# Padding that starts both operands of the large products at one remainder of 512 bytes

## The chip, the cores and the metric

One core of a Trainium2 chip runs the kernel as one program. The metric is device microseconds (us) of one execution. The five engines are TensorE (PE in the rows; its weight loads are PEld), VectorE (DVE), ScalarE (ACT), GpSimd (POOL) and SyncE (SP). On-chip memory is addressed by bytes along each of 128 partitions; a tile starts at the same byte in each of them.

## What is computed

The reference, cut to its three stages:

```python
attn = softmax(q @ mean8(k).T * scale)          # 8 x 8 heads, 576 rows, 72 pooled keys
x = attn @ mean8(v)                             # to 4608 tokens x 512
idx = argmax(xn @ en.T / tau)                   # one of 8 experts for each token
out[idx == e] = gate * (relu(x[idx == e] @ w1[e]) @ w2[e])   # 512 -> 1024 -> 512
h = out @ w_in                                  # 512 -> 2048
return (h * cos(h)) @ w_out                     # 2048 -> 512
```

## The kernel before

Each large product is done three times over split operands: a float32 operand is cast to the tile `hi` (type fp32r), and `lo` is what the cast lost; hi·hi, lo·hi and hi·lo are summed in PSUM. A product instruction has a stationary operand of 128 x 128 elements, which a weight load (LDWEIGHTS) brings in, and a moving operand of 128 x 512 elements. Each product has a weight load of its own, and TensorE fetches the next one while a product runs.

After attention (to about 215 us) come 41 items of 128 tokens of one expert. `gemm1` (line 707) multiplies the transposed tokens `xh`/`xl` (stationary) with expert weights in `slot` (moving): 24 products for an item. `t_h` (719) transposes the result, and `gemm2` (730) multiplies `h0h`, `h0l`, `h1h`, `h1l` (stationary) with `slot` (moving), again 24. The order on TensorE is gemm1 of item i, four transposes of the next item's tokens (686), gemm2 of item i-1, eight transposes of item i's result. VectorE makes the hi and lo tiles (679, 680), the relu (710) and, between items, converts feed-forward weights.

From about 737 us the feed-forward stage runs over 9 groups of 512 tokens with 16 steps in each, 144 steps. A step has 12 products in `ff1` (854): the stationary operand is a piece of `slot` (the first weights), the moving one is `x2`, the group's transposed tokens. Then come 12 products of `ff2` (880) for the step two before: `gh`/`gl` are stationary, `slot` (the second weights) is moving. Between them `act` makes gh and gl of a step: ScalarE writes `u` (864), VectorE takes off the whole turns through `nr` (865, 866), ScalarE takes the sine (867), VectorE multiplies with the result in PSUM (868) and writes gh and gl (869, 870). x2 alternates between two places, `x2a` for even groups and `x2b` for odd ones.

Where the built program places these tiles, in bytes of the partition, before and after the change:

| tile | used as | start before | remainder of 512 | start after | remainder of 512 |
|---|---|---|---|---|---|
| slot (131072 bytes) | moving in gemm1, gemm2, ff2; stationary in ff1 | 21632 | 128 | 21632 | 128 |
| xh, xl | stationary in gemm1 | 175456, 177504 | 352, 352 | 175744, 177792 | 128, 128 |
| h0h, h0l, h1h, h1l, gh, gl | stationary in gemm2 and ff2 | 152704 and on by 2048 | 128 | the same | 128 |
| x2a | moving in ff1, even groups | 200672 | 480 | 200704 | 128 |
| x2b | moving in ff1, odd groups | 175456 | 352 | 175744 | 128 |
| u (two), nr | work tiles of act | 196576, 198624, 194528 | 480 | 196224, 198272, 194176 | 128 |
| h | relu's result, transposed by t_h | 179552 | 352 | 179840 | 128 |

All pieces of these operands lie at multiples of 512 bytes from the start of their tile, so a piece has the remainder of its tile. u, nr and h are not padded themselves: they lie beside tiles that are.

Of the kernel before, what the change touches and what calls it, by code (L numbers as in the profile page):

```python
# [8 lines left out]
F32 = mybir.dt.float32  # L9
F32R = mybir.dt.float32r  # L10
# [12 lines left out]
def attention_moe_ffn_kernel(  # L23
# [21 lines left out]
    KC = DM // 128  # L45
    FC1 = F1 // 128
# [3 lines left out]
    XW = DM + 2  # L50
# [8 lines left out]
    def pool(name, bufs, es=ctx, **kw):  # L59
        return es.enter_context(tc.tile_pool(name=name, bufs=bufs, **kw))  # L60

    const = pool("const", 1)
    wes = ExitStack()
    rawp = [pool("rawa", 3, side="right"), pool("rawb", NB - 3, wes, side="right")]
    dram = pool("dram", 1, space=DRAM)
# [3 lines left out]
    def bank(i, name):  # L69
        return psp[0].tile([128, 512], F32, tag=f"p{i}", name=name)  # L70
# [38 lines left out]
    W_GROUP = "expert_weights"  # L109
    sem_raw = [tc.alloc_semaphore(f"raw{i}") for i in range(NB)]  # L110

# [3 lines left out]
    def w_load(j, eng=nc.scalar):  # L115
        e, c = order[j]
        t = rawp[j % NB > 2].tile([128, QW], F32, tag="raw", name="raw")
        src = (w1 if c < 4 else w2)[e].rearrange("(p k) n -> p (k n)", p=128)
        d = eng.dma_start(t, src[:, (c % 4) * QW:(c % 4 + 1) * QW])
        d.then_inc(sem_raw[j % NB], 16)  # L120
        tc.no_tile_sem_insts.add(d.ins.name)
        tc.add_to_no_dep_group(f"raw_load{j}", d.ins)
        raws[j] = t

    def w_hi(slot, j):
        e, c = order[j]
        s = ((e + 1) % 2) * SLOT
        hi = slot[:, s + c * QW:s + (c + 1) * QW]
        lo = slot[:, s + HALF + c * QW:s + HALF + (c + 1) * QW]
        nc.scalar.wait_ge(sem_raw[j % NB], 16 * (j // NB + 1))  # L130
        i = nc.scalar.activation(hi, raws[j], AF.Copy)  # L131
        tc.declare_no_dep(i.ins, group=f"raw_load{j}", reason="waits for the load's own semaphore")
        tc.declare_fence(i.ins, group=f"raw_load{j}")
        tc.add_to_no_dep_group(W_GROUP, i.ins)
        raws[j] = raws[j], hi, lo
# [72 lines left out]
    def scatter(n):  # L208
        xt = XT.pop(n)
        nc.gpsimd.tensor_copy(xt[:, DM:XW], GT[:, n, :])  # L210
        apart("xv_rows", nc.gpsimd.indirect_dma_start(
            out=xv, out_offset=bass.IndirectOffsetOnAxis(ap=DESTI[:, n:n + 1], axis=0),
            in_=xt, in_offset=None,
        ))


    def phase_a(es, xtp, zero):
# [277 lines left out]
        def step(n):  # L495
# [88 lines left out]
            if n >= 0 and n % 9 == 8:  # L584
                for j in range(NB // 4):
                    w_load(n // 9 * (NB // 4) + j)
# [63 lines left out]
    def experts_and_feed_forward(slot, wes):  # L650
        htp = pool("hTp", 1)
# [3 lines left out]
        xtp = pool("xTp", 1, bes)  # L655
# [15 lines left out]
            else:  # L671
                d = nc.sync.dma_start(X[i], xv[0:128, :])

        def halves(pl, tg):
            return [pl.tile([128, 4, 128], F32R, tag=tg + t, name=tg + t) for t in "hl"]

        def split(p, hi, lo):
            pv = p.rearrange("p (k n) -> p k n", k=4)
# [141 lines left out]
        Y, X2 = {}, {}  # L820
# [6 lines left out]

        def t_y(g, r, b):
            if r == 0:
                X2[g] = x2p[g % 2].tile([128, 2, KC, 512], F32R, tag="x2", name="x2")  # L830
            n = g * 4 + r
            t, x2 = Y.pop(n), X2[g][:, :, :, r * 128:(r + 1) * 128]
            p = bank(b, "pt2")
            for kk in range(KC):
                nc.tensor.transpose(p[:, kk * 128:(kk + 1) * 128], t[:, 0:DM].rearrange("p (c k) -> p k c", k=KC)[:, kk, :], ident)  # L835
            pv = p.rearrange("p (k n) -> p k n", k=KC)

            def rest():
                nc.vector.tensor_copy(x2[:, 0], pv)
                nc.vector.tensor_tensor(x2[:, 1], pv, x2[:, 0].bitcast(F32), ALU.subtract)  # L840
                nc.vector.tensor_copy(POS[:, n:n + 1], t[:, DM:DM + 1])

            return rest
# [14 lines left out]
        def act(n):  # L858
            p = PH.pop(n)
            u = cp.tile([128, 512], F32, tag="u", name="u")  # L860
            nr = cn.tile([128, 512], F32, tag="nr", name="nr")
            gh = htp.tile([128, 4, 128], F32R, tag=f"h{n % 2}h", name="gh").rearrange("p a n -> p (a n)")
            gl = htp.tile([128, 4, 128], F32R, tag=f"h{n % 2}l", name="gl").rearrange("p a n -> p (a n)")
            nc.scalar.activation(u, p, AF.Identity, scale=1.0 / TWO_PI_EXACT, bias=quarter)  # L864
            nc.vector.tensor_scalar(nr, u, MAGIC, MAGIC, op0=ALU.add, op1=ALU.subtract)  # L865
            nc.vector.tensor_tensor(u, u, nr, ALU.subtract)  # L866
            nc.scalar.activation(u, u, AF.Sin, scale=TWO_PI)  # L867
            nc.vector.tensor_tensor(u, u, p, ALU.mult)  # L868
            nc.vector.tensor_copy(gh, u)  # L869
            nc.vector.tensor_tensor(gl, u, gh.bitcast(F32), ALU.subtract)  # L870
            G[n] = (gh, gl)
# [29 lines left out]
        while todo:  # L901
            scatter(todo.pop(0))
        for j in range(WH):
            w_hi(slot, j)
        for f in f2:
            f()
        for j in range(WH, NB):
            w_hi(slot, j)
# [12 lines left out]
        for j in range(NB, 2 * NB - 1):  # L921
            if j == NB + 4:
                conv_load(0)
                conv_load(1)
            w_load(j, nc.sync)
        xT = halves(xtp, "x")
        hT = [halves(htp, f"h{n}") for n in range(FC1 // 4)]
        h = hp.tile([128, F1], F32, tag="h", name="h")
        t_x(0)
        phase_x(slot, NB, 16)  # L930
# [23 lines left out]
        gl, gl2 = (const.tile([128, 2], F32, name=t) for t in ("gl", "gl2"))  # L954
# [20 lines left out]
        x2p = [pool("x2a", 1, side="right")]  # L975
# [4 lines left out]
        for fn in [t_y(0, r, r) for r in range(4)]:  # L980
            fn()
# [10 lines left out]
        for n in range(NS + 2):  # L992
            if n < FC2:
                wc_split(n, True)
                wc_load(n + 3)
                if 3 <= n + 2 < FC2:
                    wc_split(n + 2, False)
            rest = None
            if n < NS:
                g, f = seq[n]  # L1000
                ff1(n)
                if g + 1 < NG:
                    if f == 3:
                        y_load(g + 1)
                    if f in (6, 8, 10, 12):
                        rest = t_y(g + 1, (f - 6) // 2, 7)
            if n >= 2:
                ff2(n - 2)
                if seq[n - 2][1] == FC2 - 1:
                    store(seq[n - 2][0])  # L1010
            if n < NS:
                act(n)
            if rest:
                rest()

    with tc.manual_schedule():
        zero = pool("zp", 1, wes, side="right").tile([128, XW], F32, name="zero")
        with ExitStack() as xes:
            xtp = pool("xtp", 18, xes, side="right")
            nc.vector.memset(zero, 0.0)  # L1020
            with ExitStack() as es:
                phase_a(es, xtp, zero)
        psp.append(pool("ps", 1, space=PSUM))
        slot = pool("slots", 1).tile([128, 2 * SLOT], F32R, name="slot")
        experts_and_feed_forward(slot, wes)


KS, KT = (0, 2, 4), (1, 4, 6)
NB = 8
WH = 3  # L1030
PF = 6
PI, PT, PB = 1, 3, 31
# [38 lines left out]
```

## Time and profile before

| | before |
|---|---|
| median of three runs | 1571.97 us (1570.59 to 1572.10) |
| the profiled execution | 1571.06 us, span 1569.0 us |
| granted TensorE clock, mean over the span | 0.985 |
| TensorE products | 1498.5 us busy, 96% of the span |
| VectorE | 1061.0 us, 68% |
| ScalarE, GpSimd | 425.1 us, 348.4 us |

The span runs from the first to the last instruction; 2.06 us of the execution's time lie outside it. Product records overlap, since a product's record holds its latency and the next one starts before it ends: the distance from start to start is what a product costs in a dense stretch.

### The profile page before, as it was taken

The numbers are of one execution on the slowest core, as the hardware profiler recorded it, in microseconds if no ns is written. First come the engines' busy times: TensorE is split into PE (matmuls) and PEld (weight loads), VectorE is DVE, ScalarE is ACT, GpSimd is POOL, SyncE is SP. The second block draws the span as 40 slices with busy tenths as digits, with TensorE's granted clock in tenths as the row PEclk, the third lists the DMA queues.
The fourth block names the chain that finished last, engine by engine and source line by source line (L and its number), as shares of the span: only waits on it lengthen the run. The fifth ranks groups of instructions, "written<-read, shape, count | busy, mean of one in ns | idle before, by whom it ended". The sixth has DMA issues, their size and how long they took to land.

```text
span 1569.0 us, 21857 instructions
## 1 busy us (share of the span) xinstructions
PE 1498.5 (96%) x7408; PEld 1248.3 (80%) x7408; DVE 1061.0 (68%) x1934; ACT 425.1 (27%) x713; POOL 348.4 (22%) x307
## 2 busy tenths in 40 slices
PE   4899959999999999999999999999999999999997
PEld 3798948878888888887778888888888888888885
DVE  4577857887888888755886655566565556656553
ACT  5687842142000000001332222222222222222221
POOL 4467776297000022001441000010001000010100
PEclk9899979999999999999999999999999999999999
DMA  8876587598333335211321010010101001010000
GB/s 261 217 222 181 174 282 237 161 294 283 107 104 101 102 118 160 87 48 42 121 74 47 1 54 1 7 48 8 47 1 54 1 14 41 7 47 1 27 1 27
DMA packets 70232, 149.43 MB, mean 95 GB/s; under 512 B 10216, under 2 KB 26600, under 8 KB 70128
## 3 DMA queue, kind: packets, MB, share of 16 engines
q1 hardware_dynamic: 55568, 97.62, 20.7%
q10 hardware_dynamic: 8800, 31.48, 6.5%
q0 software_dynamic: 5760, 18.92, 3.2%
q8 instruction: 68, 1.11, 0.3%
q14 instruction: 36, 0.29, 0.1%
HBM read 107.82 MB, written 40.17 MB: 94 GB/s over the span
## 4 chain that ended last, share of the span: by engine, by line
issue 39%; PE 12%; POOL 2%; DVE 0%; ACT 0%; POOLq 0%; ACTq 0%
PE ph L854 6%; PE po L880 6%; POOL out_dram L891 2%; PE pt L835 0%; PE py L730 0%; DVE gl L870 0%; DVE gh L869 0%; ACT L867 0%; PE pth L719 0%; POOLq L890 0%; DVE u L868 0%; ACT u L864 0%; ACT u L867 0%; ACT o L888 0%; POOLq L891 0%
## 5 line engine op out<-in xcount | busy, mean ns | idle before, releaser
L854 PE MATMUL ph<-x,slot 128*128 128x512 f32 x1728 | 427.6, 396 | 0.0
L854 PEld LDWEIGHTS ph<-x,slot 128*128 128x128 f32 x1728 | 324.7, 188 | 77.8 <-issue 0.2
L880 PE MATMUL po<-slot,gh 128*128 128x512 f32 x1152 | 382.8, 393 | 0.0
L880 PEld LDWEIGHTS po<-slot,gh 128*128 128x128 f32 x1152 | 216.7, 188 | 48.2
L880 PE MATMUL po<-slot,gl 128*128 128x512 f32 x576 | 226.4, 393 | 0.9 <-DVE gl L870 0.9
L139 POOL TENSOR_TENSOR slot<-raw,slot 128x1024 fp32r<-128x1024 f32 x60 | 142.0, 2404 | 252.7 <-ACT slot L131 247.1
L864 ACT ACTIVATE u<-ph,quarter 128x512 f32<-128x512 f32 x144 | 98.9, 686 | 352.5 <-PE ph L854 352.2
L891 POOL DMA_INDIRECT out_dram<-o,POS x36 | 37.0, 1027 | 696.6 <-ACT o L888 688.4
L707 PE MATMUL ph<-slot,xh 128*128 (+1 forms) x656 | 179.2, 405 | 4.1 <-POOLq L144 2.7
L865 DVE TENSOR_SCALAR nr<-u 128x512 f32<-128x512 f32 x144 | 62.4, 434 | 164.9 <-ACT u L864 164.9
L868 DVE TENSOR_TENSOR u<-u,ph 128x512 f32<-128x512 f32 x144 | 99.2, 689 | 100.7 <-ACT u L867 100.7
L131 ACT ACTIVATE slot<-raw 128x1024 fp32r<-128x1024 f32 x64 | 66.2, 1056 | 328.8 <-DVEq L711 237.5
L867 ACT ACTIVATE u<-u 128x512 f32<-128x512 f32 x144 | 91.1, 632 | 220.7 <-DVE u L866 220.7
L707 PEld LDWEIGHTS ph<-slot,xh 128*128 128x128 f32 x656 | 121.8, 191 | 31.8 <-DVE h1h L679 2.9
L880 PEld LDWEIGHTS po<-slot,gl 128*128 128x128 f32 x576 | 108.3, 188 | 24.6 <-DVE gl L870 2.1
L870 DVE TENSOR_TENSOR gl<-u,gh 128x512 fp32r<-128x512 f32 x144 | 112.3, 780 | 5.0
L866 DVE TENSOR_TENSOR u<-u,nr 128x512 f32<-128x512 f32 x144 | 99.9, 694 | 4.9
L730 PE MATMUL py<-slot,h0h 128*128 (+1 forms) x328 | 91.9, 402 | 0.1
L707 PE MATMUL ph<-slot,xl 128*128 (+1 forms) x328 | 91.1, 400 | 0.0
L730 PE MATMUL py<-slot,h1h 128*128 (+1 forms) x328 | 88.1, 390 | 0.0
L869 DVE CAST gh<-u 128x512 fp32r<-128x512 f32 x144 | 76.0, 528 | 14.4 <-DVE u L868 0.5
L815 POOL TENSOR_TENSOR slot<-wst,slot 128x512 fp32r<-128x512 f32 x32 | 43.1, 1368 | 183.1 <-ACT slot L811 183.1
(169 smaller groups left out, 1843.9 us busy)
## 6 DMA issues: line engine op xcount, KB each, us to landing
raw<-in_moe_w_dram ACTq DMA_DIRECT2D x57, 512.0 KB, 6.2
xb<-xv SPq DMA_DIRECT2D x43, 257.0 KB, 3.6
yv<-y SPq DMA_DIRECT2D x41, 256.5 KB, 3.2
yb<-yv SPq DMA_DIRECT2D x36, 256.5 KB, 3.4
kraw<-in_k_dram SPq DMA_DIRECT2D x12, 768.0 KB, 9.0
vraw<-in_v_dram SPq DMA_DIRECT2D x8, 1152.0 KB, 7.8
q<-in_q_dram SPq DMA_DIRECT2D x8, 1024.0 KB, 12.6
craw<-in_moe_w_in_dram SPq DMA_DIRECT2D x16, 512.0 KB, 4.5
```

The lines of the kernel that those rows point to most:

```text
L139: i = eng.tensor_tensor(lo, t, hi.bitcast(F32), ALU.subtract)
L707: mm = nc.tensor.matmul(p, a[:, kk, :], at(so, o + kk * F1 + n * 512), start=(c == 0), stop=(c == 3 * KC - 1))
L730: mm = nc.tensor.matmul(p, a[:, kk, :], at(so, o + W2O + (n * 4 + kk) * DM), start=(c == 0), stop=(c == 3 * FC1 - 1))
L854: nc.tensor.matmul(p, win[:, f, s, kk * 128:(kk + 1) * 128], x2[:, m, kk, :], start=(c == 0), stop=(c == 3 * KC - 1))
L864: nc.scalar.activation(u, p, AF.Identity, scale=1.0 / TWO_PI_EXACT, bias=quarter)
L866: nc.vector.tensor_tensor(u, u, nr, ALU.subtract)
L867: nc.scalar.activation(u, u, AF.Sin, scale=TWO_PI)
L868: nc.vector.tensor_tensor(u, u, p, ALU.mult)
L869: nc.vector.tensor_copy(gh, u)
L870: nc.vector.tensor_tensor(gl, u, gh.bitcast(F32), ALU.subtract)
L880: nc.tensor.matmul(O[g][r], a[:, r * 128:(r + 1) * 128], wout[:, f, s, :], start=(f == 0 and c == 0), stop=(f == FC2 - 1 and c == 2))
L891: apart("out_rows", nc.gpsimd.indirect_dma_start(out=out, out_offset=bass.IndirectOffsetOnAxis(ap=POS[:, g * 4 + r:g * 4 + r + 1], axis=0) ...
```

## The change

Three tiles get unused elements in front of, or behind, the part that is used, so that the used part starts at remainder 128, where slot starts. `at_word(pool, n, pad, o, tag)` allocates n + pad elements of 4 bytes and hands out n of them from element o on. xh and xl become the two halves of one tile xT (72 elements pad, 288 bytes, in front). x2b gets the same. x2a, whose memory is handed out from the top down, gets 88 elements (352 bytes) behind the used part. h0h with h0l, and h1h with h1l, become one tile each, without padding. The tile `zero` (zero rows for a buffer in device memory) comes from a pool that is given back with the attention's tiles and no longer with the expert weights' buffers.

```diff
+        def at_word(pl, n, pad, o, tag):
+            return pl.tile([128, n + pad], F32R, tag=tag, name=tag)[:, o:o + n]
+
+        def halves(pl, tg, pad, o):
+            t = at_word(pl, 1024, pad, o, tg).rearrange("p (s a n) -> p s a n", s=2, a=4)
+            return [t[:, 0], t[:, 1]]
-                X2[g] = x2p[g % 2].tile([128, 2, KC, 512], F32R, tag="x2", name="x2")
+                X2[g] = at_word(x2p[g % 2], 2 * KC * 512, *X2_AT[g % 2], "x2").rearrange("p (s k n) -> p s k n", s=2, k=KC)
-            gh = htp.tile([128, 4, 128], F32R, tag=f"h{n % 2}h", name="gh").rearrange("p a n -> p (a n)")
-            gl = htp.tile([128, 4, 128], F32R, tag=f"h{n % 2}l", name="gl").rearrange("p a n -> p (a n)")
+            gh, gl = (t.rearrange("p a n -> p (a n)") for t in halves(htp, f"h{n % 2}", *H_AT[n % 2][0::2]))
-        xT = halves(xtp, "x")
-        hT = [halves(htp, f"h{n}") for n in range(FC1 // 4)]
+        xT = halves(xtp, "xT", *X_AT)
+        hT = [halves(htp, f"h{n}", *H_AT[n][0:2]) for n in range(FC1 // 4)]
-        zero = pool("zp", 1, wes, side="right").tile([128, XW], F32, name="zero")
         with ExitStack() as xes:
+            zero = pool("zp", 1, xes, side="right").tile([128, XW], F32, name="zero")
+X_AT, H_AT, X2_AT = (72, 72), ((0, 0, 0), (0, 0, 0)), ((88, 0), (72, 72))
```

No instruction is added, removed or moved. What two tiles in one could alter is the waits, so the order is shown with them. First TensorE at gemm1 of the first item, before (ph is the result in PSUM; xh and xl the stationary operand):

```order
L707 MATMUL ph<-slot,xh 128x512 [waits DMAHW3_49,DMAHW2_49,DMAHW4_49,DMAHW1_49,DMAHW5_49,DMAHW0_49,DMAHW6_49,w1_ready,DVE_49]
L707 MATMUL ph<-slot,xh 128x512 x3
L707 MATMUL ph<-slot,xl 128x512 [waits DVE_49]
L707 MATMUL ph<-slot,xl 128x512 x3
L707 MATMUL ph<-slot,xh 128x512 x8
L707 MATMUL ph<-slot,xl 128x512 x4
L707 MATMUL ph<-slot,xh 128x512 x4
```

The same place with the change (line 707 is now 712, 686 is 691; xT holds both halves):

```order
L691 MATMUL ptx<-ident,xb 128x128 x3
L712 MATMUL ph<-slot,xT 128x512 [waits DMAHW3_49,DMAHW2_49,DMAHW4_49,DMAHW1_49,DMAHW5_49,DMAHW0_49,DMAHW6_49,w1_ready,DVE_49]
L712 MATMUL ph<-slot,xT 128x512 x3
L712 MATMUL ph<-slot,xT 128x512 [waits DVE_49]
L712 MATMUL ph<-slot,xT 128x512 x19
L691 MATMUL ptx<-ident,xb 128x128 [waits DMAHW0_49,PE_49]
```

The first product still waits for VectorE once and the fifth, which is the first to read the lo half, once more; no product waits for the whole tile. In the rest of the program each engine's instructions and waits stand as before, up to names and line numbers.

## Rows read from the trace of the kernel before

**Rows 1.** The page: span, engines, granted clock in 40 slices of the span.

```profile
span 1569.0 us, 21857 instructions
...
PE 1498.5 (96%) x7408; PEld 1248.3 (80%) x7408; DVE 1061.0 (68%) x1934; ACT 425.1 (27%) x713; POOL 348.4 (22%) x307
...
PEclk9899979999999999999999999999999999999999
```

**Rows 2.** Windows by stage: busy us (instructions) of each engine, clock, DMA share, GB/s.

```profile
370.00:500.00 130.00, 130.00 (x628) 108.34 (x627) 113.68 (x179) 4.25 (x4) 11.77 (x5) 1.00 0.40 129
...
850.00:1558.00 708.00, 708.00 (x3112) 576.89 (x3111) 413.27 (x722) 172.28 (x264) 29.69 (x29) 1.00 0.06 20
```

**Rows 3.** Waits of TensorE: releaser, total us, times, longest us.

```profile
PE ptx L686 <- DMA xb<-xv: 11.9, 1, 11.9
...
PE ph L707 <- POOLq L144: 2.7, 1, 2.7
...
PE po L880 <- DVE gl L870: 0.9, 1, 0.9
PE ph L707 <- DVE xh L679: 0.8, 1, 0.8
```

**Rows 4.** The chain that ended last: start, us, engine, tile, line, count.

```profile
921.43 2.76 PE po L880 x12
924.19 2.81 PE ph L854 x12
```

**Rows 5.** Windows, line 854 alone: TensorE busy us (instructions), clock, DMA, GB/s.

```profile
850.00:1558.00 708.00, 368.36 (x1488) 1.00 0.06 20
```

**Rows 6.** The page, fifth part: busy us, mean ns of one, idle before.

```profile
L854 PE MATMUL ph<-x,slot 128*128 128x512 f32 x1728 | 427.6, 396 | 0.0
```

**Rows 7.** Timeline of TensorE, feed-forward stage: start, us, line, operands, count.

```profile
1210.65 0.39 PE L880 MATMUL po<-slot,gh 128*128 128x512 f32 x1
...
1211.81 0.62 PE L880 MATMUL po<-slot,gh 128*128 128x512 f32 x2
...
1213.40 2.96 PE L854 MATMUL ph<-x,slot 128*128 128x512 f32 x12
```

**Rows 8.** Timeline of TensorE, expert stage, one item and part of the next.

```profile
603.10 1.04 PE L719 MATMUL pth<-ident,h 128*128 128x128 f32 x8
603.89 1.18 PE L707 MATMUL ph<-slot,xh 128*128 x4
...
605.85 2.03 PE L707 MATMUL ph<-slot,xh 128*128 x8
...
609.59 0.64 PE L686 MATMUL ptx<-ident,xb 128*128 128x128 f32 x4
609.98 1.18 PE L730 MATMUL py<-slot,h0h 128*128 x4
611.00 1.08 PE L730 MATMUL py<-slot,h0l 128*128 x4
...
613.74 0.61 PE L730 MATMUL py<-slot,h1l 128*128 x2
```

**Rows 9.** Timeline of ScalarE in the feed-forward stage.

```profile
1210.85 0.69 ACT L864 ACTIVATE u<-ph,quarter 128x512 f32<-128x512 f32 x1 [2.29 <-PE ph L854]
1212.76 0.63 ACT L867 ACTIVATE u<-u 128x512 f32<-128x512 f32 x1 [1.22 <-DVE u L866]
```

**Rows 10.** Timeline of VectorE in the feed-forward stage.

```profile
1211.57 0.43 DVE L865 TENSOR_SCALAR nr<-u 128x512 f32<-128x512 f32 x1 [1.03 <-ACT u L864]
...
1213.42 0.69 DVE L868 TENSOR_TENSOR u<-u,ph 128x512 f32<-128x512 f32 x1 [0.70 <-ACT u L867]
1214.22 0.43 DVE L869 CAST gh<-u 128x512 fp32r<-128x512 f32 x1
1214.68 0.69 DVE L870 TENSOR_TENSOR gl<-u,gh 128x512 fp32r<-128x512 f32 x1
```

**Rows 11.** Waits of VectorE from 370 to 737 us.

```profile
DVE y L734 <- PE py L730: 46.3, 29, 3.7
```

More of the change, by code (lines that the diff above doesn't have):

```diff
@@ L672, in load @@
                 d = nc.sync.dma_start(X[i], xv[0:128, :])
-        def halves(pl, tg):
-            return [pl.tile([128, 4, 128], F32R, tag=tg + t, name=tg + t) for t in "hl"]
+        def at_word(pl, n, pad, o, tag):
[3 more added lines that the diff above has]
+            return [t[:, 0], t[:, 1]]
         def split(p, hi, lo):
```

## The prediction

> **What bounds the kernel now.** I read the page first. TensorE's products are busy for 96% of a span of 1569.0 us and no other engine is above 68%; the granted clock is at its upper level (the 2.4 GHz one) in nearly all slices after the attention [rows 1]. Then the windows by stage: in the expert stage TensorE is busy for 130.00 us of 130.00, in the feed-forward stage for 708.00 of 708.00, both at a granted clock of 1.00 [rows 2]. Then its waits. The longest is 11.9 us, once, for the first tokens; weights cost 2.7 us once, gl 0.9 us once, xh 0.8 us once [rows 3]. So nothing that the change touches waits for another engine. The chain that ended last says the same: in its later part it is runs of twelve products, ff1 and ff2 by turns [rows 4]. What a product costs from start to start is therefore the whole matter in both stages.
>
> **The same product has two prices.** In the chain, twelve ff1 products take 2.81 us and twelve ff2 products 2.76 us [rows 4], 234 and 230 ns each, although shape, type and clock are the same. Over the stage: ff1 was busy 368.36 us with 1488 products [rows 5], in 124 runs of twelve. A run is eleven distances and one record of 0.396 us [rows 6], so a distance is (368.36/124 - 0.396)/11 = 0.2341 us. Inside ff2, seven distances from 1211.81 to 1213.40 us are 1.59 us, 227.1 ns each, while the five from 1210.65 to 1211.81 are 232 ns [rows 7]. ScalarE writes u from 1210.85 to 1211.54 [rows 9] and VectorE writes nr from 1211.57 to 1212.00 [rows 10], so the dear ones lie beside those.
>
> The expert stage has the same two prices. In gemm1, 16 products from 605.85 to 609.59 take 3.74 us, 233.8 ns each; in gemm2, 12 from 611.00 to 613.74 take 2.74 us, 228.3 ns each [rows 8]. This pair is the cleaner evidence: both have a split activation as the stationary operand and slot as the moving one, VectorE works beside both, and of what the program fixes I find one difference that ff1 and ff2 share with them. gemm2 and ff2 have both operands at remainder 128 of 512 bytes; gemm1 has 352 against 128, ff1 128 against 480 or 352. The PSUM banks don't divide them so: bank 6 takes results of gemm2 and of ff1. The change gives the two dear products the remainders of the two cheap ones.
>
> **What the change costs and brings, part by part.**
>
> *ff1.* 144 runs of 12, 1728 products, now at 234.1 ns. Afterwards they lie between the undisturbed 227.1 ns and the 232 ns of the disturbed part of ff2. I place them by cover. Twelve ff2 products have 230 ns on average beside 0.69 + 0.43 + 0.69 + 0.63 = 2.44 us of ScalarE and VectorE work on u and nr (line 866, whose row is not shown, taken as long as 868); ff1 has beside it lines 868, 869 and 870 of VectorE, 0.69 + 0.43 + 0.69 = 1.81 us [rows 9, 10]. So 227.1 + 2.9 x 1.81/2.44 = 229.2 ns, and the gain is 4.9 ns x 1728 = 8.5 us. Bounds: 227.1 ns gives 12.1 us, 232 ns gives 3.6 us.
>
> *gemm1.* 41 items of 24, 984 products, from 233.8 ns to gemm2's 228.3 ns: 5.5 ns x 984 = 5.4 us. Bounds: 227.1 ns gives 6.6 us; 230 ns, ff2's average, gives 3.7 us.
>
> *What can take it back in the expert stage.* A shorter item leaves VectorE less time. An item is shorter by 24 x 5.5 ns = 0.13 us, and VectorE waited for gemm2's result 29 times between 370 and 737 us, 46.3 us in all [rows 11], 1.6 us a time. The cover is twelve times what is taken from it; I charge nothing. If it were gone, 41 x 0.13 = 5.4 us, the whole gain of gemm1, would go with it.
>
> *Two tiles in one.* The waits stand as before, on the halves, so the first product is not held until the lo half is written. Had it been, a VectorE instruction of 0.69 us [rows 10] would have been late once an item and a step at most; the order shows that it is not, and I charge nothing.
>
> *u, nr and h move along.* u and nr come to remainder 128 without being asked to. No row shows these instructions at another place. If their disturbance of ff2 went with the distance, ff2 would fall from 230 to 227.1 ns: 2.9 ns x 1728 = 5.0 us more. If they disturbed every ff2 product, 232 ns throughout: 2 ns x 1728 = 3.5 us lost. I take zero, between the two, and keep both ends. For h, eight transposes of it (remainder 352) take 0.79 us from 603.10 to 603.89 and four of the tokens 0.39 us from 609.59 to 609.98 [rows 8]: 99 and 98 ns, from operands at different places. I charge nothing.
>
> *zero.* Its tile lies where it lay, and was read long before the place is used again. Nothing.
>
> Sum: 1569.0 - 8.5 - 5.4 = 1555.1 us of span, with 2.06 us outside it 1557.2 us. The profiled execution is 0.9 us below the median of the runs, so 1558.1 us against 1571.97.
>
> **A rule that speaks against it.** The row first: gemm1 and gemm2, alike in shape, role and clock, are 5.5 ns apart [rows 8]. The Trainium skill, "TensorE: Matmul & The Clock Gate", Part 2 (the step on LDWEIGHTS), says that TensorE has two independent read ports into on-chip memory, and that loading the next weights takes no read bandwidth from the running product. By that rule the place of one operand against the other is of no account, and the sum would be zero. The trace does not agree as far as it goes, since a difference is there; but no run yet shows that the place causes it. It is the third rival below.
>
> **The rivals.**
>
> *The neighbours' disturbance goes too.* Place matters for every engine's access, and u and nr at remainder 128 leave ff1, ff2 and gemm1 at 227.1 ns: 12.1 + 5.0 + 6.6 = 23.7 us, about 1548. For it: the dear part of ff2 coincides with writes of u and nr at 480. Against it: 870 writes gl at 128 and 867 writes u at 480, and seven products beside 866 and 867 are undisturbed.
>
> *Only one of the two products gains,* because what hurts the other is its role and not its place (in ff1 alone slot is stationary). gemm1 alone: 1566.6; ff1 alone: 1563.5. For it: ff1 and ff2 differ in roles as well. Against it: gemm1 and gemm2 do not, and show the same two prices.
>
> *The change does not do what it says.* Two read ports that do not meet: 1572, within 0.2%. For it: the remainders are the only evidence, in two pairs of products that also stand at different points of the order. Against it: the price follows the remainders in both stages.
>
> *Slower.* u and nr are brought to the remainder of the products' own operands, and ScalarE's and VectorE's accesses to them, which now raise five ff2 products of twelve from 227.1 to 232 ns, then raise every product of the feed-forward stage by those 5 ns, so that ff1 has nothing of its padding either: ff2 goes from 230 to 232 ns, ff1 from 234.1 to 239 ns. That is 2 x 1728 + 5 x 1728 ns = 12.1 us lost, less gemm1's 5.4 us: 1578.7. It decides the sign where the 3456 products of the stage rise by 5.4 us/3456 = 1.6 ns on average. Against it: 868 to 870 use u, gh and gl beside ff1 already, two of them at 128, and ff1's 234.1 ns is hardly above gemm1's 233.8 with other work beside it.
>
> **How the numbers follow.** Forecast as summed, with its bounds (3.6 + 3.7 = 7.3 us gained to 12.1 + 6.6 = 18.7 us gained, 1553.3 to 1564.7): 0.66. Everything undisturbed, 1547 to 1553: 0.10. One product only: 0.10, half of it either way. No effect: 0.08. Slower: 0.06. The range from 1548 to 1565 holds the forecast, most of the second case and ff1 alone: 0.66 + 0.09 + 0.05 = 0.80. A change of 0.2%, 3.1 us, is about what a measurement of this kernel can tell from none. Faster by more: 0.66 + 0.10 + 0.10 = 0.86; within: 0.08; slower: 0.06.
>
> **What would show it.** In the chain after, runs of twelve ff1 products at 2.72 to 2.78 us instead of 2.81, those of ff2 near 2.76; in the timeline, 16 gemm1 products in some 3.65 us instead of 3.74; attention, transposes and waits as before. The place has no part if ff1 and gemm1 keep 234 ns. It is the role if only one of them moves. u and nr count if the first five distances of an ff2 run change from 232 ns. I am wrong altogether if TensorE shows new waits for xT, gh or gl.

## The result and the profile after

The changed kernel takes 1552.01 us (median of three, 1551.92 to 1552.96) against 1571.97: the ratio is 0.9877, with a 95% interval from 0.9855 to 0.9900. A later measurement of it gave 1550.60 against 1571.01, ratio 0.9870 (0.9853 to 0.9886). Forecast was 1558.1, range 1548 to 1565.

The page of the changed kernel, span and engines, answers to [rows 1]:

```profile
span 1550.1 us, 21857 instructions
...
PE 1475.7 (95%) x7408; PEld 1245.6 (80%) x7408; DVE 1059.3 (68%) x1934; ACT 425.3 (27%) x713; POOL 347.6 (22%) x307
```

TensorE's products are busy for 22.8 us less (1498.5 to 1475.7); the other engines do the same work. Where the 18.9 us of span went is read from the first product of gemm1 and the first of ff1. The timeline of TensorE before, then after (start in us, busy us, line, operands, count):

```profile
215.09 2.08 PE L707 MATMUL ph<-slot,xh 128*128 128x512 f32 x4 [0.84 <-DVE xh L679]
...
737.39 8.64 PE L854 MATMUL ph<-x,slot 128*128 128x512 f32 x36
```

```profile
216.60 1.65 PE L712 MATMUL ph<-slot,xT 128*128 128x512 f32 x3 [0.84 <-DVE xT L684]
...
732.83 2.53 PE L859 MATMUL ph<-x,slot 128*128 128x512 f32 x10
```

Up to gemm1 the changed kernel is 1.51 us later; attention has its tiles where it had them, and the repeated run reaches gemm1 at 214.50 us, earlier than the kernel before, so this is scatter. The expert stage takes 516.23 us instead of 522.30, 6.1 less. From ff1 to the end of the span it is 817.3 instead of 831.6, 14.3 less. Together that is 20.4 us, less the 1.5.

In the feed-forward stage the windows for ff1's line alone (busy us, instructions, clock, DMA, GB/s) answer to [rows 5], and the timeline of TensorE in group 2 to [rows 4, 7]:

```profile
850.00:1535.00 685.00, 354.73 (x1476) 1.00 0.07 21
```

```profile
933.91 2.88 PE L859 MATMUL ph<-x,slot 128*128 128x512 f32 x12
936.63 2.88 PE L884 MATMUL po<-slot,h 128*128 128x512 f32 x12
939.35 2.88 PE L859 MATMUL ph<-x,slot 128*128 128x512 f32 x12
```

With the working of [rows 5], (354.73/123 - 0.389)/11 = 0.2268 us: an ff1 product costs 226.8 ns instead of 234.1 (0.389 us is the mean record of an ff1 product on the page after). Twelve of ff1 and twelve of ff2 both take 2.72 us, 226.7 ns each, and behind ff1 there is no dear part at the head of ff2 any more.

The expert stage, as in [rows 8]:

```profile
600.55 5.73 PE L712 MATMUL ph<-slot,xT 128*128 x24
606.12 0.63 PE L691 MATMUL ptx<-ident,xb 128*128 128x128 f32 x4
606.50 5.75 PE L735 MATMUL py<-slot,h 128*128 x24
612.09 1.04 PE L724 MATMUL pth<-ident,h 128*128 128x128 f32 x8
```

The 24 products of gemm1 take 5.57 us (600.55 to 606.12) instead of 5.70 (603.89 to 609.59 in [rows 8]), those of gemm2 5.59.

The waits of TensorE answer to [rows 3]:

```profile
PE ph L712 <- POOLq L144: 3.0, 1, 3.0
...
PE pt L840 <- PE ph L859: 1.9, 2, 1.0
PE pt L840 <- issue: 1.5, 1, 1.5
...
PE py L735 <- DVE xT L684: 1.1, 1, 1.1
...
PE po L884 <- DVE h L874: 1.1, 1, 1.1
```

The same view of the repeated run has one line that bears on these:

```profile
PE py L735 <- POOLq L144: 1.4, 1, 1.4
```

One wait is new: 1.1 us, once, ahead of the first gemm2. The view puts it down to VectorE's cast to xT, a tile that gemm2 does not read; in the repeated run the wait at this place is 1.4 us and stands under GpSimd's report that an expert's weights are ready (L144), for which the program makes gemm2 wait. So it is a wait for weights and not for xT. The wait of gemm1 for weights grew by 0.3 us (2.7 to 3.0). What else grew is in group 0 of the feed-forward stage, whose weights and first rows come while it runs: the transposes' waits were 1.5 and 1.2 us before, the one for gl 0.9 [rows 3]. That is 0.9 us given back.

### The profile page after: what moved, and what is told of

Its sections match the earlier page's. It is cut to its first block, busy times and chain, and to the rows that moved or that the text cites. A ratio compares the mean times of both kernels' runs of the same rounds, so it can differ in the third digit from the quotient of the medians.

```text
span 1550.1 us, 21857 instructions
## 1 busy us (share of the span) xinstructions
PE 1475.7 (95%) x7408; PEld 1245.6 (80%) x7408; DVE 1059.3 (68%) x1934; ACT 425.3 (27%) x713; POOL 347.6 (22%) x307
## 4 chain that ended last, share of the span: by engine, by line
issue 39%; PE 12%; POOL 2%; DVE 0%; ACT 0%; POOLq 0%; ACTq 0%
PE ph L859 6%; PE po L884 6%; POOL out_dram L895 2%; PE pt L840 0%; PE py L735 0%; DVE h L874 0%; DVE h L873 0%; ACT L871 0%; PE pth L724 0%; POOLq L894 0%; DVE u L872 0%; ACT u L868 0%; ACT u L871 0%; ACT o L892 0%; POOLq L895 0%
## 5 line engine op out<-in xcount | busy, mean ns | idle before, releaser
L884 PE MATMUL po<-slot,h 128*128 128x512 f32 x1728 | 419.9, 392 | 1.1 <-DVE h L874 1.1
L859 PE MATMUL ph<-x,slot 128*128 128x512 f32 x1728 | 415.1, 389 | 0.0
L859 PEld LDWEIGHTS ph<-x,slot 128*128 128x128 f32 x1728 | 324.3, 188 | 67.5 <-issue 0.2
L884 PEld LDWEIGHTS po<-slot,h 128*128 128x128 f32 x1728 | 322.0, 188 | 68.8 <-DVE h L874 2.9
L712 PE MATMUL ph<-slot,xT 128*128 (+1 forms) x984 | 236.3, 396 | 4.4 <-POOLq L144 3.0
L735 PE MATMUL py<-slot,h 128*128 (+1 forms) x984 | 235.1, 394 | 1.1 <-DVE xT L684 1.1
L712 PEld LDWEIGHTS ph<-slot,xT 128*128 128x128 f32 x984 | 182.9, 189 | 42.0 <-DVE h L685 3.2
L735 PEld LDWEIGHTS py<-slot,h 128*128 128x128 f32 x984 | 182.1, 188 | 38.0 <-DVE xT L684 1.3
L874 DVE TENSOR_TENSOR h<-u,h 128x512 fp32r<-128x512 f32 x144 | 112.4, 781 | 5.0
L873 DVE CAST h<-u 128x512 fp32r<-128x512 f32 x144 | 76.1, 528 | 14.5 <-DVE u L872 0.5
L715 DVE TENSOR_SCALAR h<-ph 128x512 f32<-128x512 f32 x82 | 53.4, 683 | 22.6 <-PE ph L712 22.6
L398 PE MATMUL pav<-vaug,atT 96*128 96x146 f32 (+1 forms) x480 | 63.4, 295 | 0.6 <-DVE vaug L313 0.3
```

What stands on the lines that cost most here:

```text
L712: mm = nc.tensor.matmul(p, a[:, kk, :], at(so, o + kk * F1 + n * 512), start=(c == 0), stop=(c == 3 * KC - 1))
L735: mm = nc.tensor.matmul(p, a[:, kk, :], at(so, o + W2O + (n * 4 + kk) * DM), start=(c == 0), stop=(c == 3 * FC1 - 1))
L859: nc.tensor.matmul(p, win[:, f, s, kk * 128:(kk + 1) * 128], x2[:, m, kk, :], start=(c == 0), stop=(c == 3 * KC - 1))
L884: nc.tensor.matmul(O[g][r], a[:, r * 128:(r + 1) * 128], wout[:, f, s, :], start=(f == 0 and c == 0), stop=(f == FC2 - 1 and c == 2))
```

## The experiments

Every kernel is the changed one with the edit shown; unless said otherwise the edit is to the line of constants. A distance says how many bytes the start of x2 (moving in ff1) or of xT (stationary in gemm1) lies past that of slot, as a remainder of 512. In the table ahead of the prediction x2a's start after the change is wrong: 200704 would be remainder 0. The built program has x2a at 200320, just behind the second u (198272 and 2048 bytes), which is remainder 128 as stated. Products are called dear where twelve of ff1 or ff2 take more than 2.72 us, or 24 of gemm1 more than 5.57. Theories: **distance** (the two operands' places against each other), **own place** (an operand off a multiple of 64 or 128 bytes is dear by itself), **neighbours** (u and nr near the operands), and **no part** (the two reads don't meet).

**xT back.**

```diff
-X_AT, H_AT, X2_AT = (72, 72), ((0, 0, 0), (0, 0, 0)), ((88, 0), (72, 72))
+X_AT, H_AT, X2_AT = (0, 0), ((0, 0, 0), (0, 0, 0)), ((88, 0), (72, 72))
```

> The changed kernel with xT back at remainder 352 (h, the conversion tiles and y0 move back with it), all else at 128. If the place of gemm1's stationary operand against slot is the cause there: gemm1's products go from some 228 ns back to 234, 984 x 5.5 ns = 5 to 6 us more than the changed kernel, about 1557.5; ff1 and ff2 keep 227 ns. If the gain came from the feed-forward tiles alone, or if xT's place has no part: 1552.

1556.91 us (1556.67 to 1557.40), ratio to before 0.9909 (0.9893 to 0.9926): 4.4 to 4.9 us above the two kernels measured beside it whose operands agree (1552.53 and 1552.02, below). The timeline of TensorE in the expert stage:

```profile
604.24 5.86 PE L712 MATMUL ph<-slot,xT 128*128 x24
609.93 0.63 PE L691 MATMUL ptx<-ident,xb 128*128 128x128 f32 x4
```

24 gemm1 products take 5.69 us again; ff1 and ff2 stay at 2.72 for twelve. So xT's place alone is worth gemm1's share.

**x2 back, u and nr left at 128.**

```diff
-X_AT, H_AT, X2_AT = (72, 72), ((0, 0, 0), (0, 0, 0)), ((88, 0), (72, 72))
+X_AT, H_AT, X2_AT = (72, 72), ((0, 0, 0), (0, 0, 0)), ((88, 88), (72, 0))
```

> The changed kernel with x2a back at 480 and x2b at 352, while u and nr stay at 128. If the place of ff1's moving operand is the cause: ff1 back from 227 to 234 ns, 1728 x 7.4 ns = 12 to 13 us more, about 1565, with ff2 near its price after. If the work tiles u and nr made ff1 cheap: ff1 stays at 227 ns and the time near 1552.

1565.28 us (1564.54 to 1568.41), ratio 0.9970 (0.9956 to 0.9984), some 13 us above those two. The timeline of TensorE, an odd group and then an even one:

```profile
843.45 2.96 PE L859 MATMUL ph<-x,slot 128*128 128x512 f32 x12
846.25 2.91 PE L884 MATMUL po<-slot,h 128*128 128x512 f32 x12
848.99 2.96 PE L859 MATMUL ph<-x,slot 128*128 128x512 f32 x12
...
934.23 2.98 PE L859 MATMUL ph<-x,slot 128*128 128x512 f32 x12
937.05 2.92 PE L884 MATMUL po<-slot,h 128*128 128x512 f32 x12
939.81 2.98 PE L859 MATMUL ph<-x,slot 128*128 128x512 f32 x12
```

ff1 is dear again, 2.80 us for twelve in odd groups (distance 224) and 2.82 in even ones (352). The telling lines are ff2's: 2.74 (846.25 to 848.99) and 2.76 us (937.05 to 939.81), dear again as before the change, although u and nr lie where the changed kernel has them. The dear head of ff2 came back with the x2 tiles, which no ff2 product reads.

**u and nr back, operands left.**

```diff
-X_AT, H_AT, X2_AT = (72, 72), ((0, 0, 0), (0, 0, 0)), ((88, 0), (72, 72))
+X_AT, H_AT, X2_AT = (72, 72), ((0, 0, 0), (0, 0, 0)), ((128, 40), (72, 72))
```

> The changed kernel with u and nr back at remainder 480, all product operands at 128. If the operands' place alone counts: ff1 227 ns, ff2 as after, time within 1 us of 1552. If the neighbours' place is what freed ff2 (and ff1) of the disturbance: runs of twelve ff2 products go back from 2.72 to 2.74 to 2.76 us and ff1's above 2.72, 2 to 6 us more, 1554 to 1558.

1552.02 us (1550.40 to 1553.87), ratio 0.9879 (0.9863 to 0.9896). The timeline of TensorE in group 2:

```profile
933.26 2.88 PE L859 MATMUL ph<-x,slot 128*128 128x512 f32 x12
935.98 2.88 PE L884 MATMUL po<-slot,h 128*128 128x512 f32 x12
938.70 2.88 PE L859 MATMUL ph<-x,slot 128*128 128x512 f32 x12
```

2.72 us for both with u and nr at 480, as before the change. With the run above this settles it: the place of u and nr has no part, and ScalarE's and VectorE's work on them, beside which the dear ff2 products stood, does not by itself make a product dear.

**All operands at 352, slot too.**

```diff
-        slot = pool("slots", 1).tile([128, 2 * SLOT], F32R, name="slot")
+        slot = pool("slots", 1).tile([128, 2 * SLOT + 56], F32R, name="slot")[:, 56:]
-X_AT, H_AT, X2_AT = (72, 72), ((0, 0, 0), (0, 0, 0)), ((88, 0), (72, 72))
+X_AT, H_AT, X2_AT = (72, 72), ((0, 0, 0), (0, 0, 0)), ((32, 0), (72, 72))
```

> Every operand of the large products, slot included, at remainder 352, with u and nr there too. If the difference of the two remainders decides: all products as cheap as in the changed kernel, 1552. If an operand is dear by itself where its start is no multiple of 64 or 128 bytes (352 and 480 are none, 128 is one): all products at 234 ns or above, that is ff1 and gemm1 back and ff2 and gemm2 worse too, 5424 x some 6 ns, 1575 to 1590.

1552.53 us (1550.11 to 1553.78), ratio 0.9883 (0.9867 to 0.9900). The timeline of TensorE in group 2:

```profile
934.59 2.88 PE L884 MATMUL po<-slot,h 128*128 128x512 f32 x12
937.31 2.88 PE L859 MATMUL ph<-x,slot 128*128 128x512 f32 x12
```

2.72 us, and so it is in odd groups and gemm1 (24 products in 5.57 us). All are cheap, at a place that is no multiple of 64 bytes. The own place has no part; the distance decides.

**How far is far.** Four kernels, one execution each, set other distances; the kernel before took 1570.92 us beside them. x2a (even groups), x2b (odd groups) and xT can each stand for a distance in one run. The four new lines are in the order of the runs.

```diff
-X_AT, H_AT, X2_AT = (72, 72), ((0, 0, 0), (0, 0, 0)), ((88, 0), (72, 72))
+X_AT, H_AT, X2_AT = (104, 104), ((0, 0, 0), (0, 0, 0)), ((88, 4), (104, 104))
+X_AT, H_AT, X2_AT = (8, 8), ((0, 0, 0), (0, 0, 0)), ((88, 64), (88, 88))
+X_AT, H_AT, X2_AT = (40, 40), ((0, 0, 0), (0, 0, 0)), ((88, 8), (40, 40))
+X_AT, H_AT, X2_AT = (88, 88), ((0, 0, 0), (0, 0, 0)), ((216, 112), (120, 120))
```

> Slot at remainder 128, x2a 16 bytes past it (even groups of ff1), x2b 128 past it (odd groups), xT 128 past it. If anything but equal remainders of 512 is dear: 2.80 to 2.82 us for twelve ff1 products in every group, gemm1 at 233 to 234 ns, as before the change, about 1571. If only the remainder of 128 counts: odd groups and gemm1 stay cheap (2.72 us, 228 ns), even ones alone are dear, about 1559.

1567.12 us. The timeline of TensorE, odd group (x2b 128), then even (x2a 16):

```profile
844.47 2.95 PE L859 MATMUL ph<-x,slot 128*128 128x512 f32 x12
847.26 2.90 PE L884 MATMUL po<-slot,h 128*128 128x512 f32 x12
...
934.86 2.94 PE L859 MATMUL ph<-x,slot 128*128 128x512 f32 x12
937.64 2.91 PE L884 MATMUL po<-slot,h 128*128 128x512 f32 x12
```

> x2a 256 bytes past slot's remainder, x2b 64 past it, xT 256 past it. Equal remainders of 512 needed: all three dear, about 1571. Remainder of 256 or of 128 counts: even groups and gemm1 cheap, odd groups dear, about 1558. Remainder of 64 counts: all cheap, 1552.

1554.82 us. Odd group (64) with the ff2 run behind it, then even (256):

```profile
842.76 2.93 PE L859 MATMUL ph<-x,slot 128*128 128x512 f32 x12
845.52 2.93 PE L884 MATMUL po<-slot,h 128*128 128x512 f32 x12
848.29 2.93 PE L859 MATMUL ph<-x,slot 128*128 128x512 f32 x12
...
932.78 2.88 PE L859 MATMUL ph<-x,slot 128*128 128x512 f32 x12
935.50 2.88 PE L884 MATMUL po<-slot,h 128*128 128x512 f32 x12
```

> x2a 32 bytes past slot's remainder, x2b and xT 384 past it (128 short of it). Equal remainders of 512 needed: all dear, about 1571. Remainder of 128 counts: odd groups and gemm1 cheap, even groups dear, about 1559. If the price grows with the distance: even groups between 2.72 and 2.80 us.

1569.53 us. Odd group (384), then even (32):

```profile
844.73 2.96 PE L859 MATMUL ph<-x,slot 128*128 128x512 f32 x12
847.52 2.90 PE L884 MATMUL po<-slot,h 128*128 128x512 f32 x12
...
929.66 2.97 PE L859 MATMUL ph<-x,slot 128*128 128x512 f32 x12
932.47 2.92 PE L884 MATMUL po<-slot,h 128*128 128x512 f32 x12
```

> x2a 448 bytes past slot's remainder (64 short of it), x2b 192 past it, xT 64 past it. Equal remainders of 512 needed: all dear, about 1571. Remainder of 64 counts: all cheap, 1552. If the price depends on the distance: the three differ from one another, and a distance may turn out cheaper than 2.72 us for twelve.

1568.16 us. Odd group (192), then even (448):

```profile
843.90 2.96 PE L859 MATMUL ph<-x,slot 128*128 128x512 f32 x12
846.71 2.90 PE L884 MATMUL po<-slot,h 128*128 128x512 f32 x12
...
934.50 2.96 PE L859 MATMUL ph<-x,slot 128*128 128x512 f32 x12
937.30 2.90 PE L884 MATMUL po<-slot,h 128*128 128x512 f32 x12
```

Twelve ff1 products take the time from the start of an L859 row to that of the L884 row behind it. 16, 32, 64, 128, 192, 384 and 448 are all dear, between 2.76 and 2.81 us; 256 is as cheap as 0. gemm1 agrees: its 24 products take 5.66 us with xT at 128, 5.57 at 256, 5.66 at 384 and 5.68 at 64. So the remainder of 256, not of 512, is what has to be equal. 128 and 384, which are the same in 256, cost the same (2.79 us both), as do 192 and 448 (2.80 to 2.81). xT is the stationary operand: where it lies 64 past slot, the moving operand lies 192 of 256 past it. Counted that way round, as in ff1, gemm1's 5.68 belongs with ff1's dear 192 and not with its cheaper 64.

**256 everywhere.**

```diff
-X_AT, H_AT, X2_AT = (72, 72), ((0, 0, 0), (0, 0, 0)), ((88, 0), (72, 72))
+X_AT, H_AT, X2_AT = (8, 8), ((0, 0, 0), (0, 0, 0)), ((88, 64), (8, 8))
```

> x2a, x2b and xT all at remainder 384, 256 bytes from the remainder 128 of slot, gh and gl; h moves to 384 too. If equal remainders of 256 are enough: ff1 2.72 us for twelve in every group, gemm1 228 ns, 1552 as the changed kernel. If equal remainders of 512 are needed: 234 ns for both, about 1571. If the cheap 256 was a matter of one tile in the sweep: only part of it, 1557 to 1565.

1550.77 us (1549.98 to 1551.62), ratio 0.9870 (0.9854 to 0.9887), the same as the changed kernel beside it. The timeline of TensorE in group 2:

```profile
932.74 2.88 PE L859 MATMUL ph<-x,slot 128*128 128x512 f32 x12
935.46 2.88 PE L884 MATMUL po<-slot,h 128*128 128x512 f32 x12
```

2.72 us for twelve; the odd groups are no different.

**One element off, and 16 bytes short.**

```diff
-X_AT, H_AT, X2_AT = (72, 72), ((0, 0, 0), (0, 0, 0)), ((88, 0), (72, 72))
+X_AT, H_AT, X2_AT = (72, 72), ((0, 0, 0), (0, 0, 0)), ((88, 1), (4, 4))
```

> x2a one element (4 bytes) past slot's remainder, x2b 16 bytes short of it (240 past it, counted in 256), xT equal. If the price is a step at any difference: both near 2.78 us for twelve, 1566. If it grows with the distance in either direction: x2a near 2.73, x2b near the 2.78 of 16 bytes past. If only whole blocks of 16 or 32 bytes count: x2a stays at 2.72.

1565.57 us, one execution. The timeline of TensorE, odd group (240), then even (4):

```profile
841.92 2.88 PE L884 MATMUL po<-slot,h 128*128 128x512 f32 x12
844.64 2.96 PE L859 MATMUL ph<-x,slot 128*128 128x512 f32 x12
847.44 2.88 PE L884 MATMUL po<-slot,h 128*128 128x512 f32 x12
...
929.71 3.00 PE L859 MATMUL ph<-x,slot 128*128 128x512 f32 x12
932.56 2.90 PE L884 MATMUL po<-slot,h 128*128 128x512 f32 x12
```

A single element costs most of all distances tried: 2.85 us for twelve (929.71 to 932.56), 237 ns each. The price does not grow with the distance, and the guesses of a slope and of blocks both fall. Of the guess of a step this much holds: every distance tried but 0 and 256 is dear, though not equally. At 240, ff1 takes 2.80 us and yet ff2 before it takes 2.72 (841.92 to 844.64): not every dear run leaves ff2 a dear head.

**Token rows at remainder 128 too.** A try at more: the rows that the transposes read.

```diff
-                X[i] = xp.tile([128, XW], F32, tag="x", name="xb")
+                X[i] = xp.tile([128, 576], F32, tag="x", name="xb")[:, 48:48 + XW]
...
-X_AT, H_AT, X2_AT = (72, 72), ((0, 0, 0), (0, 0, 0)), ((88, 0), (72, 72))
+X_AT, H_AT, X2_AT = (48, 48), ((0, 0, 0), (0, 0, 0)), ((88, 0), (48, 48))
```

(Three other uses of these tiles likewise; the rows of the first feed-forward group get the 576 elements without the offset.)

> The changed kernel, and the token rows that are transposed (xb, yb) padded to 2304 bytes, so that each starts at remainder 128 of 256 as the identity does. If the place of a transpose's operand sets its price, and what gemm2 and ff2 take over from the transposes ahead of them: the transposes before gemm2 fall from some 119 to 109 ns and the first gemm2 products from 231 to 236 ns to 227, 312 x 10 ns + 984 x 2 ns = 5 us less, 1547. If strided reads or the other engines make these products dear: 1552.

1550.87 us (1549.73 to 1551.47) against 1550.60 for the changed kernel beside it. The timeline of TensorE in the expert stage:

```profile
604.02 0.63 PE L691 MATMUL ptx<-ident,xb 128*128 128x128 f32 x4
604.41 5.73 PE L735 MATMUL py<-slot,h 128*128 x24
609.98 1.04 PE L724 MATMUL pth<-ident,h 128*128 128x128 f32 x8
```

Four transposes still take 0.39 us (604.02 to 604.41), 24 gemm2 products 5.57 instead of 5.59. The rows' place makes no difference that counts; these transposes read them with a step, and what sets their price is open.

**The changed kernel again.**

> The changed kernel once more, as the measure for the runs beside it: 1552, within 0.2%, by either theory.

1550.60 us (1550.23 to 1550.81), ratio 0.9870 (0.9853 to 0.9886): within 0.1% of the first measurement.

## Why the prediction was right, and where it was off

*What bounds the kernel* held: but for one wait of 1.1 us for weights TensorE waits for nothing new, and what products cost from start to start is what the time gained. That the operands' places against each other set the price held as well.

*The sum* of the gains came out too small: 13.9 us forecast, 20.0 measured. 1552.01 us lies below the sum's own bounds (1553.3 to 1564.7) and in the case "everything undisturbed" (1547 to 1553), which had a chance of 0.10. That the stated range holds the time is owed to its having taken in most of that rival, not to the sum.

*gemm1* was sized right: 5.4 us forecast; 0.13 us an item in the timeline is 5.3 us for 41 items, and putting xT back costs 4.4 to 4.9 us.

*ff1* is the term that was mis-sized: 8.5 us forecast, (234.1 - 226.8) x 1728 = 12.6 us measured, just beyond the forecast's own bound of 12.1; putting x2 back costs 13 us, ff2's share in it. The step that failed is the placing by cover: I took the dear head of ff2 for a disturbance by ScalarE's and VectorE's work on u and nr, and gave ff1 its part of the same. No such disturbance shows: beside the same work ff1 and ff2 both run at 226.7 ns. In the timeline before, the dear products stood beside that work, and they also stood right behind ff1; the run with x2 back and the one with u and nr back tell the two apart, and it was ff1. A dear run is, in most cases, followed by some dear products of the next kind, even though their own operands agree; why, no run shows.

*u, nr and h* were charged nothing, with 5.0 us gained to 3.5 lost as bounds. Their place is worth nothing; the eight transposes of h take 0.79 us (612.09 to 612.88 in the timeline after), as before. ff2 did gain, but through ff1: the feed-forward stage's 14.3 us are ff1's 12.6 less the 0.9 given back in group 0, and the 2.6 left over are ff2's. So the sign that the prediction set for u and nr, that the first five distances of an ff2 run change from 232 ns, came without its cause. Of the expert stage's 6.1 us, gemm1's 5.3 leave 0.8 that I have assigned to no row; from the first product of gemm1 to the first of ff1 it is 515.5 us in the run with x2 back and 517.4 in the one with 256 everywhere, both with gemm1 cheap, so 0.8 is within scatter.

*Two tiles in one, zero, and VectorE's cover* cost nothing, as forecast: VectorE still waits for gemm2's result 29 times between 370 and 732 us, 43.6 us in all, against 46.3 [rows 11].

*The rivals.* "The neighbours' disturbance goes too" named the price that came, 227.1 ns, with a cause that the run with u and nr back refutes. "One of the two products" falls: each gained by its own tile. "Slower" falls with the changed kernel itself: ff2 is cheaper with u and nr at 128, not dearer. "Two ports that do not meet" falls: xT and x2, moved alone, each brought its price back, 5 ns a product in gemm1 (5.69 us for 24 against 5.57) and 7 to 8 in ff1 (2.80 and 2.82 us for twelve against 2.72). By the rule of the Trainium skill, "TensorE: Matmul & The Clock Gate", Part 2, that loading the next weights takes no read bandwidth from the running product, the place should have had no part. The measurements decide against that consequence here; whether the two reads meet at the memory or somewhere else in TensorE, no run shows.

The best version found is the changed kernel; only its 512 is more than is needed.

## What to carry to other kernels

Where one kind of product costs some ns more than another of the same shape, type and clock, compare the two operands' start addresses before blaming the engines that happen to work beside it. Here the stationary and the moving operand of fp32r products of 128 x 128 by 128 x 512 had to start at the same remainder of 256 bytes to run at 226.7 ns, and padding did that at no cost in time. A dear stretch that stands next to other work is not yet caused by it: move one suspect at a time.

## What was not expected of the hardware

- As far as tried, the price of an ff1 product goes by the distance's remainder of 256 bytes and is lowest only at remainder 0: 226.7 ns at 0 and 256, 230 ns at 64, 232 to 235 ns at 16, 32, 128, 192, 224, 240, 352, 384 and 448, and 237 ns at 4.
- A dear run reaches into the next one: ff2's twelve took 2.74 to 2.76 us behind ff1 at distances 224 and 352, 2.72 behind ff1 at 0, 256 and 240, with operands of their own that agreed in every case. How far it reaches does not go with the price: behind 64, where ff1 is the cheapest of the dear ones, ff2 took the most, 2.77 us (845.52 to 848.29).
